# An attention-and-gate kernel: the fourth head pair's scores, maximum and exponentials moved ahead of batch 1's transposes in the opening list, and one copy of v rows moved from a DMA queue to GpSimd

## The chip, the core and the metric

The kernel runs on one core of a Trainium2 chip. The time is that of one execution on the device, in microseconds (us); a figure for a kernel is the median over its runs. The engines are named as in the profile: PE (TensorE matmul), PEld (TensorE weight load), DVE (VectorE), ACT (ScalarE), POOL (GpSimd), SP (SyncE, which here only issues DMAs).

## What is computed

The inputs are `q`, `k`, `v` of shape (8 batches, 8 heads, 576 positions, 64) and two weight matrices. Attention looks back over a window of 64 positions; its result, with the heads side by side, goes through two matrix products with a cosine gate between them.

```python
scores = q @ k.T / sqrt(64)                       # per batch and head
mask = (rel >= 0) & (rel < 64)                    # rel = row position - column position
scores = where(mask, scores, -1e9)
attn = exp(scores - max(scores)); attn = attn / (sum(attn) + 1e-9)
x = (attn @ v), heads side by side                # 4608 rows x 512
h = x @ w_in                                      # 512 -> 2048
out = (h * cos(h)) @ w_out                        # 2048 -> 512
```

## The kernel before

The 4608 rows are cut into nine macro-tiles of 512 rows (`MT`). For macro-tiles 1 to 8 a loop writes down the two big products (L458 for `x @ w_in`, L611 for the product with `w_out`), and a planner (`at`, `pump`) drops the attention steps of later tiles in between. Macro-tile 0 and the attention of batches 0 and 1 have no such cover yet. Their order is written out by hand in the string `FIRST`: a list of step names, emitted one after the other (L575). The list is the program order on each engine: every instruction that a step emits goes to the end of its engine's queue, and an engine takes its queue strictly in order, waiting on semaphores where data or buffers are not ready.

The names of the steps that matter here (`p` is a pair of heads, 0 to 3; `g` is 0 for the first four blocks of 64 positions of a pair, 1 for the next four):

| step | what it does | engine, line |
|---|---|---|
| `Lq1.x`, `Lk1.x`, `Lv0.x`, `Lwi.x` | loads of q and k of batch 1, of v of batch 0 (128 rows each), of a quarter of `w_in` | issued by POOL, L149, L172, L188 |
| `tq.p`, `tk.p` / `Tq.p`, `Tk.p` | 18 transposes of q or k of batch 0 / of batch 1 into PSUM | PE, L200 |
| `pq.p`, `pk.p` / `Pq.p`, `Pk.p` | copies of those transposes to SBUF, the last letter names the engine (`a` ACT, `d` DVE) | L121, L222, L224 |
| `s.p.g.bank` | scores of a group of four blocks: two matmuls that put the mask, then eight of q and k | PE, L304, L311 |
| `m.p.g` | row maximum of the group | DVE, L321 |
| `e.p.g` | four exponentials, each with its row sum | ACT, L338 |
| `i.p.g` | reciprocal of the row sums | DVE, L348 |
| `n.p.g.p` | exponentials times reciprocals, giving the weights `w` | POOL, L355 |
| `w.p.g`, `c.p.g` | four transposes of `w`, and their copy to SBUF | PE, L371; DVE or ACT, L121 |
| `zA`, `zB.0`, `zB.1`, `zC` | copies of half a v block into the odd slots of the v tile, 64 partitions each; `zB.0` and `zB.1` cover two slots (64x1024). The letter: `d` DVE, `s` a DMA from SP (L183), `p` POOL | |
| `v.a.g`, `x.a.g` | weights times v for two pairs (`a` is 0 or 1), and the copy into `xT` | PE, L408; L121 |
| `h.g.f.bank` | eight matmuls of `x @ w_in` | PE, L422 |
| `tb`, `S.g.f` | ACT's table load for the sine, and the sines | ACT, L453, L428 |
| `Gs.n`, `Gm.n` | scores and maximum of groups of batch 1 (numbers 9 to 12 here) | PE, L311; DVE, L326 |

`v.0.1` reads slots 3 and 5 of the v tile, whose lower halves `zB.0` fills and whose upper halves `zB.1` fills. `zB.0` needs the third and the fourth load of v (`Lv0.2`, `Lv0.3`), `zB.1` the second and the third. `zA` and `zC` fill slots 1 and 7. Waits between steps come from the data and from the buffers: the PSUM tiles with the tag `t` go round over three banks, and the scores, `h` and output tiles name their bank.

On PE the list runs, from the last transposes of batch 0 to the first `h`: `Tq.0 Tk.0 s.3.0 Tq.1 Tk.1 s.2.1 Gs.10 Gs.9 w.0.0 w.1.0 Gs.12 w.2.0 w.3.0 v.0.0 s.3.1 v.1.0 Gs.11 w.0.1 w.1.1 h.0.0 h.0.1 w.2.1 h.0.2 v.0.1 w.3.1 h.0.3`. On POOL, after the loads: `n.1.0 n.0.0 n.2.0 n.3.0 n.0.1 n.1.1 n.2.1 Lwi.3 n.3.1`.

Of the kernel before, what the change touches and what calls it, by code (L numbers as in the profile page):

```python
# [10 lines left out]
def _safe_warn(msg, *a, **kw):  # L11
# [30 lines left out]


FIRST = (
# [18 lines left out]
)  # L63


# [585 lines left out]
```

## Time and profile before

| | |
|---|---|
| median of 3 runs | 306.01 us (305.65 to 306.83) |
| the profiled execution | 306.57 us, of which the span from the first to the last instruction is 304.8 us |
| PE busy | 293.2 us, 96% of the span |
| ACT, DVE, POOL busy | 233.7, 217.4, 195.8 us |
| DMA moved | 41.44 MB, 136 GB/s in the mean |

Times in the views are microseconds from the start of the span. A row of the timeline gives the start, the time that its instructions took together, engine, line, operation, `out<-in`, shape and count; in brackets stands the idle time of the engine just before it and what ended it. Rows of equal operations that follow each other are merged. Matmuls are pipelined, so that the starts, not the durations, tell how fast PE goes. A wait for several semaphores is put down to the one that the profile saw last.

### The profile page before, as it was taken

What the parts mean: (1) busy time and instruction counts of PE and PEld (TensorE: products, weight loads), DVE (VectorE), ACT (ScalarE), POOL (GpSimd) and SP (SyncE); (2) the same over time, 40 slices, a digit from 0 to 9 for tenths busy, and PEclk for the clock granted to TensorE, in tenths of its full rate; (3) what the DMA queues carried; (4) which work ended last, traced back from release to release, by engine and by line L of the source; (5) the groups of instructions that cost most, each with busy time, mean ns of one, the idle gap of its engine ahead of it and who ended that gap; (6) DMA issues with size and microseconds to landing.
All of it is one profiled execution on the core that took longest, in us unless ns stands there. A gap on an engine that the chain in (4) does not pass through costs nothing.

```text
span 304.8 us, 8261 instructions
## 1 busy us (share of the span) xinstructions
PE 293.2 (96%) x2840; PEld 154.4 (51%) x2840; DVE 217.4 (71%) x868; ACT 233.7 (77%) x783; POOL 195.8 (64%) x226
## 2 busy tenths in 40 slices
PE   3789999999999999999999999999999999999995
PEld 3667854644455445444544444444544454454443
DVE  3797888898888877787678867886778677236701
ACT  5998699878986799779976998699869986116500
POOL 8899568986999579985998599769804930000000
PEclk9999999999999999999999999999999999999999
DMA  7999999999979995999999999999996852011011
GB/s 144 175 203 184 196 189 142 103 132 169 232 115 115 228 147 80 106 153 233 133 116 150 223 138 109 128 235 148 107 123 147 139 120 98 0 71 69 3 69 69
DMA packets 158186, 41.44 MB, mean 136 GB/s; under 512 B 146944, under 2 KB 153408, under 8 KB 158144
## 3 DMA queue, kind: packets, MB, share of 16 engines
q0 software_dynamic: 100192, 18.06, 80.8%
q1 hardware_dynamic: 57808, 22.66, 40.7%
q8 instruction: 22, 0.36, 0.5%
q14 instruction: 20, 0.16, 0.2%
q10 hardware_dynamic: 144, 0.20, 0.2%
HBM read 36.70 MB, written 9.44 MB: 151 GB/s over the span
## 4 chain that ended last, share of the span: by engine, by line
PE 90%; DVE 3%; DMA 2%; POOL 2%; ACT 1%; issue 1%; POOLq 0%
PE h_ps L458 37%; PE out_ps L611 36%; PE out_ps L441 5%; PE h_ps L422 4%; PE s_ps L289 3%; PE o_ps L390 3%; DMA k<-in_k_dram 2%; PE tq_ps L203 1%; PE out_ps L470 1%; DVE negm L321 1%; POOL q L149 1%; PE s_ps L311 1%; POOL k L149 1%; ACT e L338 0%; DVE wT L121 0%
## 5 line engine op out<-in xcount | busy, mean ns | idle before, releaser
L458 PE MATMUL h_ps<-xT,w_in 128*128 128x512 bf16 x512 | 115.1, 379 | 0.2
L611 PE MATMUL out_ps<-w_out,gT 128*128 128x512 bf16 x496 | 110.0, 379 | 0.0
L600 DVE TENSOR_TENSOR gT<-h_ps,sin 128x512 bf16<-128x512 f32 x128 | 85.1, 688 | 29.3 <-ACT sin L597 28.7
L338 ACT ACTIVATE e<-s,negm 128x128 f32<-128x128 f32 (+1 forms) x256 | 97.2, 382 | 1.7 <-POOL v L121 1.0
L597 ACT ACTIVATE sin<-h_ps 128x512 f32<-128x512 f32 x128 | 73.8, 598 | 31.4 <-PE h_ps L458 30.8
L355 POOL TENSOR_TENSOR w<-e,rden 128x512 bf16<-128x512 f32 (+1 forms) x68 | 69.3, 1033 | 30.8 <-DVE rden L348 25.0
L458 PEld LDWEIGHTS <-w_in 128*128 128x128 bf16 x512 | 48.9, 98 | 54.7
L611 PEld LDWEIGHTS <-gT 128*128 128x128 bf16 x496 | 47.4, 98 | 56.1
L326 DVE CUSTOM_DVE_ANT_0 s<-s_ps,mask 128x128 f32<-128x128 f32 (+1 forms) x256 | 56.1, 277 | 1.7 <-PE s_ps L311 1.4
L338 ACT ACTIVATION_READ_ACCUMULATOR e<-s,negm 128x1 f32 x256 | 48.3, 189 | 0.0
L172 POOL DMA_DIRECT2D v<-in_v_dram x40 | 34.1, 870 | 1.0 <-DMA q<-in_q_dram 1.0
L166 POOL DMA_DIRECT2D q<-in_q_dram x36 | 28.7, 797 | 7.6 <-DMA v<-in_v_dram 2.5
L166 POOL DMA_DIRECT2D k<-in_k_dram x36 | 28.5, 792 | 6.4 <-DMA k<-in_k_dram 4.5
L121 ACT COPY out_sb<-out_ps 128x512 f32<-128x512 f32 (+1 forms) x16 | 9.0, 563 | 23.9 <-PE out_ps L611 18.4
L348 DVE RECIPROCAL rden<-den 128x4 f32<-128x4 f32 (+1 forms) x73 | 12.2, 167 | 19.4 <-ACT e L338 19.0
L121 POOL COPY v<-v 64x1536 bf16<-64x1536 bf16 (+3 forms) x16 | 22.9, 1433 | 0.4
L121 DVE COPY out_sb<-out_ps 128x512 f32<-128x512 f32 x20 | 13.7, 687 | 12.1 <-PE out_ps L611 12.0
L121 DVE CAST xT<-o_ps 128x512 bf16<-128x512 f32 x24 | 15.6, 679 | 8.6 <-PE o_ps L390 8.4
L326 DVE DVE_READ_ACCUMULATOR2_ANT negm<- 128x1 f32 x256 | 21.3, 83 | 0.1
L441 PE MATMUL out_ps<-w_out,gT 128*128 128x512 bf16 x64 | 14.8, 380 | 0.0
L422 PE MATMUL h_ps<-xT,w_in 128*128 128x256 bf16 x128 | 14.6, 273 | 0.0
L422 PEld LDWEIGHTS <-w_in 128*128 128x128 bf16 x128 | 12.3, 98 | 1.4
(67 smaller groups left out, 230.9 us busy)
## 6 DMA issues: line engine op xcount, KB each, us to landing
out_dram<-out_sb SPq DMA_DIRECT2D x16, 512.0 KB, 7.3
v<-in_v_dram POOLq DMA_DIRECT2D x32, 128.0 KB, 6.0
q<-in_q_dram POOLq DMA_DIRECT2D x36, 96.0 KB, 8.7
k<-in_k_dram POOLq DMA_DIRECT2D x36, 96.0 KB, 8.6
w_in<-in_moe_w_in_dram POOLq DMA_DIRECT2D x4, 512.0 KB, 9.2
w_out<-in_moe_w_out_dram POOLq DMA_DIRECT2D x4, 512.0 KB, 11.0
q<-in_q_dram POOLq DMA_DIRECT2D x7, 144.0 KB, 6.5
k<-in_k_dram POOLq DMA_DIRECT2D x7, 144.0 KB, 6.7
```

Source lines behind the costliest of these rows:

```text
L121: {"a": nc.scalar.copy, "p": nc.gpsimd.tensor_copy}.get(engine, nc.vector.tensor_copy)(out, in_)
L166: nc.gpsimd.dma_start(out=st[name, b][:, c].rearrange("p (h d) -> p h d", h=H), in_=src.rearrange("h p d -> p h d"))
L172: nc.gpsimd.dma_start(out=vt.rearrange("p (h d) -> p h d", h=H), in_=v[b, :, c * 128:c * 128 + n, :].rearrange("h p d -> p h d"))
L326: nc.vector.tensor_tensor_reduce(out=s[:, u, c], in0=s_ps[:, u, c], in1=mask[:, 2 - j % 2 if j else 0, c], scale=-scale if b else -1.0, sc ...
L338: nc.scalar.activation(e[:, u, c], s[:, u, c], AF.Exp, bias=negm[:, u:u + 1], scale=1.0 if n < n_first else -1.0, accum_out=den[:, u:u + 1])
L355: (nc.gpsimd if engine == "p" else nc.vector).tensor_tensor(out=w[:, 0:u], in0=e[:, 0:u], op=ALU.mult, in1=rden[:, 0:u].unsqueeze(2).to_br ...
L422: nc.tensor.matmul(out=h_ps[:, half * e:half * e + half], lhsT=w_in_sb[:, ks, ff * 128:ff * 128 + 128], rhs=st["xT", 0][:, ks, half * g:ha ...
L441: nc.tensor.matmul(out=st["out", m], lhsT=st["g", ff // 2][:, ff % 2, m * 128:m * 128 + 128], rhs=w_out_sb[:, ff], start=ff == 0, stop=ff ...
L458: nc.tensor.matmul(out=st["h", ff], lhsT=w_in_sb[:, ks, ff * 128:ff * 128 + 128], rhs=st["xT", mt][:, ks], start=start, stop=stop)
L597: nc.scalar.activation(sin, h_ps, AF.Sin, bias=math.pi / 2.0)
L600: nc.vector.tensor_tensor(out=gt[:, e], in0=h_ps, in1=sin, op=ALU.mult)
L611: nc.tensor.matmul(out=o_ps[e], lhsT=gT[ff // 2][:, ff % 2, ms * 128:ms * 128 + 128], rhs=w_out_sb[:, ff], start=ff == 0, stop=ff == n_ff - 1)
```

## The change

Four steps of the list move ahead of neighbours, and one letter changes.

- `i.0.0` goes ahead of `pk.3.d` and `m.2.0` (DVE).
- `s.3.0.0` goes ahead of `Tk.0` (PE).
- `m.3.0` goes ahead of `Pq.0.d` and `i.1.0` (DVE).
- `e.3.0` goes ahead of `Pk.0.a` (ACT).
- `zB.0.s` becomes `zB.0.p`: the copy of v rows of slots 3 and 5, lower halves, is one POOL copy of 64x1024 instead of a DMA from SP. In POOL's queue it stands between `n.3.0` and `n.0.1`; in SP's queue `zB.1` is now the first of these copies.

The instructions are otherwise the same, in number too: PE keeps its 5682, and the list is written on one line less, so that later lines of the changed kernel have numbers lower by one.

```diff
 FIRST = (
...
-    "... Tq.0 Lv0.2 pk.3.d m.2.0 e.0.1 pq.3.a i.0.0 e.1.0 Tk.0 s.3.0.0 Tq.1 e.2.0 Lv0.3 Lwi.0 "
-    "Pq.0.d i.1.0 Lwi.1 m.3.0 m.1.1 i.2.0 Pk.0.a e.3.0 Lwi.2 Tk.1 n.1.0.p s.2.1.1 Pq.1.d ..."
+    "... Tq.0 Lv0.2 i.0.0 pk.3.d m.2.0 e.0.1 pq.3.a e.1.0 s.3.0.0 Tk.0 Tq.1 e.2.0 Lv0.3 Lwi.0 m.3.0 "
+    "Pq.0.d i.1.0 Lwi.1 m.1.1 i.2.0 e.3.0 Pk.0.a Lwi.2 Tk.1 n.1.0.p s.2.1.1 Pq.1.d ..."
...
-    "... n.3.0.p i.0.1 c.1.0.d zA.1.d c.2.0.d e.2.1 zB.0.s zB.1.s n.0.1.p i.1.1 w.3.0 v.0.0 ..."
+    "... n.3.0.p i.0.1 c.1.0.d zA.1.d c.2.0.d e.2.1 zB.0.p zB.1.s n.0.1.p i.1.1 w.3.0 v.0.0 ..."
...
 )
```

35 rows, old and new, of the table FIRST are left out of this document.

## The prediction

> **What bounds the kernel now.** I read the busy times first, then everything that PE waits for in the whole span (total, times, longest).
>
> ```profile
> PE 293.2 (96%) x2840; PEld 154.4 (51%) x2840; DVE 217.4 (71%) x868; ACT 233.7 (77%) x783; POOL 195.8 (64%) x226
> ...
> PE tq_ps L200 <- DVE q L121: 4.2, 1, 4.2
> PE tk_ps L200 <- issue: 1.4, 1, 1.4
> PE tw_ps L371 <- POOL w L355: 1.1, 2, 0.9
> PE o_ps L408 <- ACT small L453: 0.6, 1, 0.6
> ```
>
> PE is the bound, and after its start its listed waits are few and all in the opening. The end therefore moves by as much as PE's last wait of the opening moves. PE's timeline shows where that is:
>
> ```profile
> 12.62 0.37 PE L200 MATMUL tk_ps<-ident,k 64*64 64x64 bf16 x11 [0.26 <-DMA k<-in_k_dram]
> 14.45 0.28 PE L200 MATMUL tk_ps<-ident,k 64*64 64x64 bf16 x7 [1.45 <-issue]
> 14.78 0.36 PE L311 MATMUL s_ps<-kT,qT 64*64 64x64 bf16 x8
> 15.77 0.75 PE L311 MATMUL s_ps<-kT,qT 64*64 64x128 bf16 x22
> 17.46 0.62 PE L371 MATMUL tw_ps<-ident,w 128*128 128x128 bf16 x8 [0.94 <-POOL w L355]
> ...
> 19.50 0.40 PE L371 MATMUL tw_ps<-ident,w 128*128 128x128 bf16 x4 [0.19 <-POOL w L355]
> ...
> 21.57 0.62 PE L371 MATMUL tw_ps<-ident,w 128*128 128x128 bf16 x8
> 22.03 1.91 PE L422 MATMUL h_ps<-xT,w_in 128*128 128x256 bf16 x16
> 23.78 0.39 PE L371 MATMUL tw_ps<-ident,w 128*128 128x128 bf16 x4
> 24.00 1.04 PE L422 MATMUL h_ps<-xT,w_in 128*128 128x256 bf16 x8
> 25.63 0.44 PE L408 MATMUL o_ps<-wT,v 128*64 128x64 bf16 x16 [0.59 <-ACT small L453]
> ```
>
> The last wait is that of `v.0.1` at 25.63. From start to start eight `h` matmuls take (23.78 - 22.03)/2 = 0.875, so PE could have begun `v.0.1` at 24.00 + 0.875 = 24.875: the wait costs 0.755, more than the 0.59 in the bracket, which counts from a pipelined end. The bracket names ACT's table load, of which `v.0.1` reads nothing. It reads v slots that SP's transfers fill; their issue, and the time to landing of the first and of the second:
>
> ```profile
> 18.17 2.18 SPq L183 DMA_DIRECT2D v<-v  x3
> v<-v SPq DMA_DIRECT2D x1, 128.0 KB, 5.7
> v<-v SPq DMA_DIRECT2D x1, 128.0 KB, 6.6
> ```
>
> `zB.0` lands at 18.17 + 5.7 = 23.9; `zB.1`, issued a third of 2.18 later, at 18.9 + 6.6 = 25.5. That is the release of 25.63.
>
> The other runner is POOL, which feeds the transposes of `w`:
>
> ```profile
> 8.98 3.53 POOL L172 DMA_DIRECT2D v<-in_v_dram  x4 [0.74 <-DMA q<-in_q_dram]
> 14.55 0.74 POOL L188 DMA_DIRECT2D w_in<-in_moe_w_in_dram  x1 [0.55 <-DMA q<-in_q_dram]
> 15.37 6.13 POOL L355 TENSOR_TENSOR w<-e,rden 128x512 bf16<-128x512 f32 x6
> 21.97 1.04 POOL L355 TENSOR_TENSOR w<-e,rden 128x512 bf16<-128x512 f32 x1 [0.47 <-DVE rden L348]
> ```
>
> Six multiplies run without a gap from 15.37 to 21.50, 1.022 each. They start when `Lwi.2` is issued, and that waits for an earlier load's landing: nothing that the change touches.
>
> **Part 1: scores, maximum and exponentials of pair 3 earlier.** The same instructions move past one another, so only the order counts. The rows of DVE and ACT there:
>
> ```profile
> 12.64 0.68 DVE L321 TENSOR_REDUCE negm<-s_ps 128x4 f32<-128x512 f32 x1
> 13.32 0.73 DVE L121 COPY qT<-tq_ps 128x576 bf16<-128x576 bf16 x1
> 13.96 0.17 DVE L348 RECIPROCAL rden<-den 128x4 f32<-128x4 f32 x1
> 15.19 1.29 DVE L321 TENSOR_REDUCE negm<-s_ps 128x4 f32<-128x512 f32 x2 [1.06 <-PE s_ps L311]
> 17.72 0.17 DVE L348 RECIPROCAL rden<-den 128x4 f32<-128x4 f32 x1
> 14.85 0.68 ACT L121 COPY kT<-tk_ps 128x576 bf16<-128x576 bf16 x1
> 15.92 0.37 ACT L338 ACTIVATE e<-s_ps,negm 128x128 f32<-128x128 f32 x1 [0.39 <-DVE negm L321]
> 17.30 0.65 ACT L121 COPY kT<-tk_ps 128x576 bf16<-128x576 bf16 x1
> ```
>
> Before, `s.3.0` stood behind the 1.45 us gap inside `Tk.0` and ran at 14.78. Now it stands in front of `Tk.0`. The gap waits for no semaphore of the program; whether it belongs to a place in PE's instruction stream, to a time near 13.0 or to `Tk.0` itself, the ten matmuls of `s.3.0` come before it (by place, with only two instructions to spare: they and one transposition with its weights fill the stretch that eleven transpositions filled). The last copy of k that they need ends as `m.2.0` begins, near 12.7, so the scores are done near 13.0.
>
> DVE: `m.2.0` ends at about 13.32, shifted to 13.4 by `i.0.0`; `m.3.0` then takes 0.59 (half of the two at 15.19, start to start 0.6) to 14.0, `Pq.0` 0.64 to 14.65, `i.1.0` follows at 14.65 instead of 13.96. `n.1.0` needs it at 15.37: 0.6 of cover, cost nothing. `i.3.0` waits for `e.3.0` and comes near 16.8 instead of 17.72.
>
> ACT: `e.3.0` runs at 14.85 in `Pk.0`'s place, (17.30 - 15.92) = 1.38 long, to 16.23; `Pk.0` and `Pk.1`, at most 0.65 each, to 16.85 and 17.4. ACT loses its 0.39 wait, but `Pk.0` is 1.4 later, and queued behind it on PE stand the scores of group 10 (from about 16.0 to 16.9) and group 9. The 14 matmuls of both are part of the 22 at 15.77 and take about 0.4, to 17.3. PE waits for POOL until 17.46 anyway: the cover is 0.15 thick. If it is gone, each further tenth shows at 17.46, but the 0.19 of idle before 19.50, where POOL is again last, takes that up.
>
> So part 1 removes PE's wait for nobody: at 17.46 and 19.50 the multiplies on POOL end last, before and after. Worth 0.0; bounds -0.05 and +0.1.
>
> **Part 2: `zB.0` on POOL.** Adds one copy to POOL's chain, before `n.0.1`. POOL's copies of v elsewhere in the kernel:
>
> ```profile
> L121 POOL COPY v<-v 64x2048 bf16<-64x2048 bf16 x5 | 9.5, 1894 | 0.3
> L121 POOL COPY v<-v 64x1024 bf16<-64x1024 bf16 x4 | 4.1, 1036 | 0.1
> L121 POOL COPY v<-v 64x512 bf16<-64x512 bf16 x2 | 2.0, 1012 | 0.1
> ```
>
> The same shape is there: 1.036. Its data (`Lv0.3`, issued last of four from 8.98, landing at 18.1 since SP's issue at 18.17 waited for it) are in place before its turn at 15.37 + 4 x 1.022 = 19.46. `n.1.1` then ends at 21.50 + 1.03 = 22.53. Queued behind: `n.2.1` ends near 23.6 instead of 23.0 (its wait of 0.47 for DVE absorbs half), PE needs it only at 24.55; `n.3.1`, after the issue of `Lwi.3` (0.8, as at 14.55), ends near 25.4 and is needed behind `v.0.1`, at 26.0. `w.0.1` has its `n.0.1` at 21.51, just in time. PE needs `n.1.1` for `w.1.1`, in the middle of the eight transposes at 21.57, that is at 21.80. With the 0.04 that lay between the end of `n.3.0` and PE's start at 19.50, `w.1.1` starts at 22.57 and `h.0.0` at 22.57 + (22.03 - 21.57)/2 = 22.80: 0.77 later than before.
>
> On SP, `zB.1` is now first and needs only the second and third v load. A load takes this long:
>
> ```profile
> v<-in_v_dram POOLq DMA_DIRECT2D x2, 128.0 KB, 6.5
> w_in<-in_moe_w_in_dram POOLq DMA_DIRECT2D x1, 512.0 KB, 12.4
> ```
>
> The third is issued at 8.98 + 2 x 0.88 = 10.74 and lands at 17.24. `zB.1` starts 1.65 earlier and lands at 17.24 + 5.7 to 6.6 = 22.9 to 23.8. PE comes to `v.0.1` at 22.80 + (24.00 - 22.03) + 0.875 = 25.65. The copy is there, the wait of 0.755 is gone, and `v.0.1` starts at 25.65 instead of 25.63.
>
> **Sum.** +0.77 (waiting for POOL) - 0.755 (no wait for SP's transfer) + 0.0 = +0.02. Behind 25.65 PE's order is the same and it has no listed wait. Against the profiled execution (306.57, span 304.8 and 1.77 around it): 306.6. The median of the runs is 0.56 lower; on that scale 306.0.
>
> **Rules weighed.** Of DVE's two equal copies of v rows, `zA`, one took 0.74, the other 0.29:
>
> ```profile
> 17.80 0.74 DVE L121 COPY v<-v 64x512 bf16<-64x512 bf16 x1
> 19.30 0.29 DVE L121 COPY v<-v 64x512 bf16<-64x512 bf16 x1
> ```
>
> The first started in the middle of POOL's third multiply and ended 0.1 after it (15.37 + 3 x 1.022 = 18.44); so the two engines can hold each other up. [...] In my sum both `zA` are done before 19.46, since DVE runs nearly 0.9 earlier from `i.3.0` on. What it would cost otherwise is the first rival.
>
> **Rivals.** *The copy on POOL is longer (0.15).* For: 64x512 took 1.012 where half the step from 1024 to 2048 leaves 1.036 - 0.43 = 0.61, so those two were held up by 0.4; against: the four of 64x1024 were not. Price 0.3 to 0.86 (as long as 2048 takes), all on PE's path at `w.1.1`: 306.3 to 306.9.
>
> *The gap catches the scores (0.05).* If the gap falls ahead of `s.3.0`'s last matmul, they end at 14.5, `m.3.0` at 15.1, and `Pq.0` and `i.1.0`, now behind `m.3.0`, at 15.9: `n.1.0` starts 0.6 late and the whole chain of POOL with it: 306.6. It decides from two instructions on.
>
> *`zB.1` lands late (0.05), the slower side.* It starts in the stage in which `w_in` loads are queued, and one of those took 12.4. From 25.65 - 17.24 = 8.4 to landing PE waits again at `v.0.1`; at 9.9 it costs 1.5, at 12.4 it costs 4.0: 307.5 to 310. Against: 5.7 and 6.6 of its own kind.
>
> *PE slows down after idling (0.03).* The same two mask matmuls took 0.62 at the start of the kernel and 0.38 soon after:
>
> ```profile
> 9.31 0.62 PE L304 MATMUL s_ps<-mask,ident 64*64 64x512 bf16 x2
> 10.49 0.38 PE L304 MATMUL s_ps<-mask,ident 64*64 64x512 bf16 x2
> ```
>
> So PE begins slower. A second slow stretch as long as the one from PE's start at 4.2 to 9.31 would cost (1 - 0.38/0.62) of 5.1 = 2.0: 308.0. Against: after the gap of 1.45 the transposes came at full pace, and the new wait at 21.80 is 0.77. [...]
>
> *A gain (0.08).* By the slope alone the copy costs 0.86, giving 305.8; if it were wholly hidden, PE would reach `v.0.1` at 24.88, giving 305.3. No row shows POOL idle there.
>
> **The numbers.** The forecast of no change has 0.64. A measurement can tell about 0.5% here, 1.53 us. Slower by more than that takes the late landing or the slow clock, 0.05 + 0.03; faster would need nearly all of PE's waits from 17.46 on (0.94 + 0.19 + 0.755), for which I leave 0.03, of the gain's 0.08; the rest, 0.89, lies within. The range goes from the gain (305.6 in its middle) less the 0.36 by which the lowest run undercut the median, to the dear copy (306.9) plus 0.3: 305.2 to 307.2.
>
> **What would show it.** Right: `s.3.0` before the gap; POOL's copy at 19.46 with about 1.03; a PE wait for POOL `w` of 0.7 before the transposes at 22.6; no wait at `v.0.1`, near 25.65; the block of 96 `h` matmuls at 27.6. Wrong: a wait left at `v.0.1`, a copy over 1.3, multiplies that start after 15.4 without a late load, or new waits after 28.

## The result, and the profile after

| | before | after |
|---|---|---|
| median of 22 runs each, side by side | 306.19 us (305.59 to 307.54) | 307.41 us (306.51 to 312.22) |
| ratio | | 1.0037 (95%: 1.0023 to 1.0052) |
| the profiled execution, and its span | 306.57 us, 304.8 us | 306.51 us, 304.7 us |
| start of the block of 96 `h` matmuls | 27.58 us | 27.67 us |

The change makes the kernel a little slower: 0.2 to 0.5%, above the 307.2 at which the forecast's range ended. The profiled execution of after is the fastest of its 22 runs, so its trace shows what the change does to the order, but not the loss. Of the 22 runs of after the one of 312.22 counts as slow (more than 1.5% above the fastest), and such runs are left out of the ratios and means here, but not out of the medians and the counts.

The busy times on the page of after:

```profile
PE 290.6 (95%) x2807; PEld 154.8 (51%) x2840; DVE 217.9 (72%) x868; ACT 233.4 (77%) x783; POOL 196.4 (64%) x227
```

What its PE waits for (total, times, longest):

```profile
PE tq_ps L199 <- DVE q L120: 4.2, 1, 4.2
PE s_ps L310 <- ACT kT L120: 1.8, 2, 1.5
PE out_ps L610 <- issue: 1.7, 11, 0.2
PE tk_ps L199 <- issue: 0.7, 1, 0.7
PE o_ps L407 <- DVE v L120: 0.5, 1, 0.5
```

POOL has one instruction more (227), the copy. The waits for POOL's `w` and at `v.0.1` (0.6 for ACT in the view of before) have left the list; a wait of 1.5 for ACT's copy of k and one of 0.5 for DVE's copy of v are new. (The 11 short "issue" gaps stand where matmul records are missing: 2807 of 2840.) PE's timeline of after, in the opening:

```profile
13.04 0.39 PE L310 MATMUL s_ps<-kT,qT 64*64 64x64 bf16 x8
...
14.17 0.44 PE L199 MATMUL tk_ps<-ident,k 64*64 64x64 bf16 x17 [0.74 <-issue]
...
17.37 0.55 PE L310 MATMUL s_ps<-kT,qT 64*64 64x128 bf16 x14 [1.46 <-ACT kT L120]
17.85 0.62 PE L370 MATMUL tw_ps<-ident,w 128*128 128x128 bf16 x8
...
20.41 0.38 PE L407 MATMUL o_ps<-wT,v 128*64 128x64 bf16 x12 [0.47 <-DVE v L120]
...
22.79 1.91 PE L421 MATMUL h_ps<-xT,w_in 128*128 128x256 bf16 x16
...
25.72 0.44 PE L407 MATMUL o_ps<-wT,v 128*64 128x64 bf16 x16
...
27.67 10.65 PE L421 MATMUL h_ps<-xT,w_in 128*128 128x256 bf16 x96
```

`s.3.0` runs at 13.04, ahead of the gap in `Tk.0`, as forecast. `w.0.0` starts at 17.85, but now PE comes to it late: until 17.37 it has waited for ACT's copy of k. `h.0.0` starts at 22.79 (forecast 22.80) and `v.0.1` at 25.72 without a wait (forecast 25.65; from the start of eight `h` matmuls to `v.0.1` it is 0.97 here, where the forecast took 0.875). Beside it POOL's and DVE's timelines of after:

```profile
15.09 4.08 POOL L354 TENSOR_TENSOR w<-e,rden 128x512 bf16<-128x512 f32 x4
19.11 1.03 POOL L120 COPY v<-v 64x1024 bf16<-64x1024 bf16 x1
20.11 2.13 POOL L354 TENSOR_TENSOR w<-e,rden 128x512 bf16<-128x512 f32 x2
...
16.91 0.35 DVE L120 COPY v<-v 64x512 bf16<-64x512 bf16 x1
19.14 1.21 DVE L120 COPY v<-v 64x512 bf16<-64x512 bf16 x1
```

The copy took the 1.03 that was forecast. DVE's second `zA`, 0.29 before, begins 0.03 after it and ends 0.2 after it: 1.21. PE's 0.47 at 20.41 is the wait for that.

### The profile page after: what moved, and what is told of

The parts are those of the page before. It is cut to its first block, busy times and chain, and to the rows that moved or that the text cites. A ratio compares the mean times of both kernels' runs of the same rounds, so it can differ in the third digit from the quotient of the medians.

```text
span 304.7 us, 8228 instructions
## 1 busy us (share of the span) xinstructions
PE 290.6 (95%) x2807; PEld 154.8 (51%) x2840; DVE 217.9 (72%) x868; ACT 233.4 (77%) x783; POOL 196.4 (64%) x227
## 4 chain that ended last, share of the span: by engine, by line
PE 92%; DVE 2%; ACT 2%; issue 2%; DMA 1%; SPq 0%
PE h_ps L457 36%; PE out_ps L610 35%; PE h_ps L421 5%; PE out_ps L440 4%; PE s_ps L288 3%; PE o_ps L389 3%; ACT e L337 1%; PE s_ps L310 1%; PE tq_ps L202 1%; PE out_ps L469 1%; DMA rows<-in_k_dram 1%; PE tk_ps L199 1%; PE tw_ps L370 1%; PE tq_ps L199 1%; DVE s L325 1%
## 5 line engine op out<-in xcount | busy, mean ns | idle before, releaser
L610 PE MATMUL out_ps<-w_out,gT 128*128 128x512 bf16 x482 | 107.3, 379 | 1.9 <-issue 1.7
L354 POOL TENSOR_TENSOR w<-e,rden 128x512 bf16<-128x512 f32 (+1 forms) x68 | 69.3, 1032 | 27.9 <-DVE rden L347 22.8
L120 POOL COPY v<-v 64x1024 bf16<-64x1024 bf16 (+3 forms) x17 | 23.9, 1408 | 0.4
L440 PE MATMUL out_ps<-w_out,gT 128*128 128x512 bf16 x60 | 14.3, 380 | 0.3 <-issue 0.2
```

Source lines behind the costliest of these rows:

```text
L120: {"a": nc.scalar.copy, "p": nc.gpsimd.tensor_copy}.get(engine, nc.vector.tensor_copy)(out, in_)
L354: (nc.gpsimd if engine == "p" else nc.vector).tensor_tensor(out=w[:, 0:u], in0=e[:, 0:u], op=ALU.mult, in1=rden[:, 0:u].unsqueeze(2).to_br ...
L440: nc.tensor.matmul(out=st["out", m], lhsT=st["g", ff // 2][:, ff % 2, m * 128:m * 128 + 128], rhs=w_out_sb[:, ff], start=ff == 0, stop=ff ...
L610: nc.tensor.matmul(out=o_ps[e], lhsT=gT[ff // 2][:, ff % 2, ms * 128:ms * 128 + 128], rhs=w_out_sb[:, ff], start=ff == 0, stop=ff == n_ff - 1)
```

## The experiments

The theories. **A**, clock and ACT: with `e.3.0` ahead of `Pk.0` PE idles for ACT, and its clock then falls in part of the runs. **B**, the copy: POOL's chain is on the path and the credit at `v.0.1` is not regular. **C**, the hold-up: POOL's copy holds up `zA.1`, and that is the loss. **D**: nothing but the spread between runs. Below, "low clock" counts runs whose granted clock, in the mean over the span, was at most 0.996.

| kernel | what it has of the change | ratio to before (95%) | low clock |
|---|---|---|---|
| after again / b / c | all | 1.0012 (0.999 to 1.0034) / 1.0013 (0.9994 to 1.0033) / 1.0013 (0.9992 to 1.0034) | 4, 6, 3 of 12 |
| before again | nothing | 0.9996 (0.9966 to 1.0027) | 1 of 12 |
| order only | the order | 1.0009 (0.9977 to 1.004) | 6 of 12 |
| copy only | the copy | 1.0009 (0.9985 to 1.0034) | 2 of 12 |
| pk first | all but `e.3.0` ahead of `Pk.0` | 1.0022 (0.9997 to 1.0047) | 0 of 12 |
| swap only | only `e.3.0` ahead of `Pk.0` | 1.0025 (1.0003 to 1.0047) | 5 of 12 |
| filled / b / c | all, and PE kept busy | 1.0001 (0.9985 to 1.0017) / 0.9999 (0.998 to 1.0018) / 1.001 (0.9989 to 1.0031) | 0, 0, 0 of 12 |
| zA early | all, `zA.1` ahead of the copy | 1.001 (0.9984 to 1.0036) | 5 of 12 |
| order, filled | the order, and PE kept busy | 1.0025 (1.0005 to 1.0046) | 1 of 12 |
| zB swap | none; `zB.1` ahead of `zB.0` on SP | 1.001 (0.999 to 1.003) | 0 of 12 |
| copy doubled | `zB.0` and `zB.1` on POOL | 1.0095 (1.0062 to 1.0128) | 5 of 9 |
| scores only | `i.0.0`, `s.3.0`, `m.3.0` early | 1.0017 (0.9991 to 1.0043) | 0 of 12 |

Single ratios of 0.1% are below what these runs tell apart; the traces and the counts carry more.

**Both kernels again, and each half alone.** The first is the changed kernel, the last the kernel before, each unedited; the two in the middle take one half of the change:

```diff
 # order only
-    "... e.2.1 zB.0.p zB.1.s n.0.1.p ..."
+    "... e.2.1 zB.0.s zB.1.s n.0.1.p ..."
 # copy only: the order of before, and in it
-    "... e.2.1 zB.0.s zB.1.s n.0.1.p ..."
+    "... e.2.1 zB.0.p zB.1.s n.0.1.p ..."
```

> The changed kernel once more, beside the others. Known so far: its median is 0.37% (1.1 us) over the kernel before, while its profiled execution, at 306.51 the lowest of its 22 runs, reaches the block of 96 h matmuls at 27.67, only 0.09 later than before. Theory O (the order on ACT and PE): with k's copies behind e.3.0, PE stands still for 1.46 in front of groups 10 and 9, and in part of the runs PE then goes slower for a stretch; theory P (the copy on POOL): DVE's second copy of v rows waits for POOL's copy, how long depends on who comes first, and in part of the runs v.0.0 is late by more than the 0.47 of the profiled one. Both expect 307.0 to 307.8 here and a spread of over 1.5; a typical execution should show the lost time, for O as matmuls at half pace, for P as a PE wait for DVE of 1 us or more near 20.

> Only the order is changed (i.0.0, s.3.0, m.3.0 and e.3.0 earlier); zB.0 stays a transfer of SP. Theory O: the loss is here, ratio 1.003 to 1.006, some granted clocks below 1. Theory P: no loss, 0.998 to 1.001, since POOL's chain is as before; by the terms of the prediction for this part 0.0 us.

> Only zB.0 goes to POOL; the order is as before. Theory P: the loss is here, ratio 1.002 to 1.006. Theory O: 0.999 to 1.001, as by the prediction's terms for this part (+0.77 of waiting for POOL, -0.755 of waiting for SP's transfer). With DVE later than in the changed kernel, its second copy of v rows may meet POOL's copy or not; the start of v.0.0 and of v.0.1 tells.

> The kernel before as a control: ratio 1.000 within 0.1%, spread below 1 us in most runs. Theory O expects granted clocks of nearly 1 in all its runs, theory P makes no difference between the clocks of the two kernels.

Neither half carries the loss alone (both 1.0009), and the repeat of after lost less than the first measurement. The traces say more. In the timeline of PE in copy only, `w.1.1` waits for POOL as forecast, and `v.0.1` waits for nothing:

```profile
22.17 0.40 PE L366 MATMUL tw_ps<-ident,w 128*128 128x128 bf16 x4 [0.57 <-POOL w L350]
22.41 1.91 PE L417 MATMUL h_ps<-xT,w_in 128*128 128x256 bf16 x16
...
25.34 0.44 PE L403 MATMUL o_ps<-wT,v 128*64 128x64 bf16 x16
```

But in the second profile of the kernel before, `v.0.1` doesn't wait either; here are PE's rows, and SP's issue:

```profile
21.42 1.91 PE L422 MATMUL h_ps<-xT,w_in 128*128 128x256 bf16 x16
...
24.18 1.05 PE L422 MATMUL h_ps<-xT,w_in 128*128 128x256 bf16 x8 [0.63 <-DVE negm L326]
25.16 0.44 PE L408 MATMUL o_ps<-wT,v 128*64 128x64 bf16 x16
...
17.42 2.43 SPq L183 DMA_DIRECT2D v<-v  x3
```

SP's transfers began at 17.42, against 18.17 in the profile on which the prediction rests, and `v.0.1` had no wait for them. The wait that this execution has instead, 0.63 for DVE's maximum, is another one.

**The swap of `e.3.0` and `Pk.0`, and PE kept busy.** For the changed kernel with the swap undone, the kernel before with the swap alone, the changed kernel with six extra mask matmuls on PE ahead of group 10's scores (they write a bank that is written again right after; nothing is left out), and the changed kernel with `zA.1` earlier:

```diff
 # pk first: of the changed kernel
-    "... i.2.0 e.3.0 Pk.0.a Lwi.2 ..."
+    "... i.2.0 Pk.0.a e.3.0 Lwi.2 ..."
 # swap only: of the kernel before
-    "... i.2.0 Pk.0.a e.3.0 Lwi.2 ..."
+    "... i.2.0 e.3.0 Pk.0.a Lwi.2 ..."
 # filled: of the changed kernel, in g_scores
-        if n == FILL[1]:
+        for _ in range(6 if n == 10 else n == FILL[1]):
 # zA early: of the changed kernel
-    "... w.1.0 c.0.0.d ... c.1.0.d zA.1.d c.2.0.d ..."
+    "... w.1.0 zA.1.d c.0.0.d ... c.1.0.d c.2.0.d ..."
```

> The changed kernel with one move undone: ACT copies k of batch 1 (Pk.0) ahead of e.3.0 again; scores and maximum of pair 3 stay early, zB.0 stays on POOL. In the three profiles with the moved order PE stood 1.3 to 1.5 us for that copy ahead of groups 10 and 9, and the granted clock was at or below 0.995 in 20 of 46 runs with that order against 7 of 59 without it. Theory O (PE's longer idle time, late start and slow stretch come from this move): PE's wait for ACT's copy of k falls below 0.6, at most 3 of 12 runs at such a clock, median 0.4 to 1 us below the changed kernel, ratio 0.998 to 1.002. Theory P (the copy on POOL is the loss): the wait goes too, but the ratio stays at 1.002 to 1.005.

> The kernel before with only e.3.0 put ahead of Pk.0 on ACT. Theory O: 4 or more of 12 runs at a clock of 0.995 or less, PE waits over 1 us for the copy of k, ratio 1.001 to 1.005. Theory P, or a theory that the early scores on PE matter: 0 to 2 such runs, ratio 0.999 to 1.001.

> The changed kernel with six more matmuls of the mask on PE (512 columns each, some 1.3 us together) ahead of group 10's scores, written where the scores overwrite them: PE is busy in the time in which it waited for the copy of k, and nothing else is added. Theory O in the form that the idle time lowers the clock: at most 2 of 12 runs at 0.995 or less, median 0.2 to 0.6 us below the changed kernel. If the slow clock had another cause, 4 or more such runs and the median of the changed kernel, 307.4, or above.

> The changed kernel with DVE's second copy of v rows (zA.1) put ahead of c.0.0, into the 0.7 to 1.0 us in which DVE waits for PE's transposes of w. In the changed kernel's profile that copy took 1.21 instead of 0.29, beside POOL's copy of v rows, and v.0.0 then waited 0.47. Theory P (the two copies hold each other up): it takes 0.3 to 0.5 here, no PE wait at v.0.0, median 0.3 to 0.6 us below the changed kernel. Theory O alone: the row gets short as well, but the runs stay as they are, 4 or more of 12 at a clock of 0.995 or less and a ratio of 1.001 to 1.004.

PE's timeline of swap only:

```profile
17.36 0.55 PE L306 MATMUL s_ps<-kT,qT 64*64 64x128 bf16 x14 [2.02 <-ACT kT L116]
17.85 0.86 PE L366 MATMUL tw_ps<-ident,w 128*128 128x128 bf16 x8
...
19.53 0.61 PE L366 MATMUL tw_ps<-ident,w 128*128 128x128 bf16 x4
19.93 0.63 PE L364 MATMUL tw_ps<-ident 128*128 128x128 bf16 x4
...
20.92 0.64 PE L403 MATMUL o_ps<-wT,v 128*64 128x64 bf16 x16
```

PE waits 2.02 for ACT's copy, and after that its rows come slower up to 21.5: four transposes 0.61 where they take 0.40, sixteen matmuls of v 0.64 instead of 0.44. With the swap undone (pk first) PE's timeline at this place is like that of before again, with the wait back at POOL:

```profile
15.25 0.83 PE L306 MATMUL s_ps<-kT,qT 64*64 64x128 bf16 x22
16.93 0.62 PE L366 MATMUL tw_ps<-ident,w 128*128 128x128 bf16 x8 [0.85 <-POOL w L350]
```

No run of pk first had the low clock; its 1.0022 is nevertheless what theory B expected, though its interval also holds no loss at all.

The view by stretches sets the granted clock beside PE's busy time: length, busy time of PE, PEld, DVE, ACT, POOL, then the granted clock, DMA share, GB/s. Swap only:

```profile
14.67:18.08 3.41, 1.39 (x43) 1.08 (x37) 2.69 (x7) 3.41 (x18) 3.35 (x4) 1.00 1.72 192
18.08:21.50 3.42, 3.06 (x43) 2.47 (x41) 2.22 (x8) 2.57 (x16) 2.92 (x4) 0.50 1.23 204
```

Filled, where the extra matmuls lie in the gap:

```profile
12.99:16.41 3.42, 2.53 (x72) 1.77 (x68) 3.42 (x9) 3.30 (x19) 3.35 (x5) 1.00 2.25 164
16.41:19.82 3.41, 3.41 (x62) 2.25 (x60) 2.52 (x10) 3.41 (x19) 3.41 (x4) 1.00 1.28 206
```

And after, the profile of the result:

```profile
14.85:18.27 3.42, 1.86 (x54) 1.54 (x51) 2.42 (x7) 3.42 (x18) 3.31 (x5) 1.00 1.72 187
18.27:21.68 3.41, 2.78 (x60) 1.98 (x60) 3.30 (x12) 2.98 (x15) 3.41 (x4) 1.00 1.22 215
```

These stretches are cut in steps of 3.413 us from the moment at which a trace's record of the clock begins. In the opening PE is slow up to a moment (11.26 in swap only, 11.44 in after; between 8.8 and 13.1 in all) at which its rows become fast and the record of the clock begins (in after b at 11.03: eighteen transposes take 0.74 at 9.83 and 0.47 at 11.11). Every later change in the records lies a whole number of stretches of 3.413 us behind that moment: in swap only 6.82 and 10.24 behind 11.26, at 18.08 and 21.50; in the first profile of before the record stands at 1.00 from 10.36 for 293.546, which is 86 stretches. In the four traces with a low clock the clock stays full for two stretches and is then 0.50 for exactly one. In the stretch just before it PE was busy 1.39 (swap only), 1.59 (order only), 1.64 (zA early) and 1.73 (after b) of 3.41; in the fifteen other traces that have the record no stretch of the opening has less than the 1.86 of after. So in these traces the drop went with how the stretches happened to fall on PE's wait. If a stretch of 3.41 is slid through a profile, the share of the positions in which it would hold less than 1.8 is an estimate of how often the clock falls; beside it stands the count of runs with the low clock:

| kernels | estimate | counted |
|---|---|---|
| `e.3.0` ahead of `Pk.0`, PE not filled (after and its repeats, order only, swap only, zA early) | 0.40, mean of seven profiles | 39 of 94 |
| before (its runs beside the experiments) | 0.11, mean of four profiles | 13 of 137 |
| copy doubled, below | 0.47, one profile | 5 of 9 |
| filled three times; order, filled | 0 | 1 of 48 |
| copy only, pk first, zB swap, scores only | 0 | 2 of 48 |

With the bound at 1.74 or 1.86, the two ends that the traces leave open, the 0.40 is 0.35 or 0.51. Theory A holds as to the clock, with the swap as the main cause and PE's idle time as the way (the low clock in 39 of 94 runs unfilled, in 1 of 48 filled). It needs no ACT: in copy doubled PE waits for POOL (1.12 and 0.60), and before has the gap inside `Tk.0`, with which its first profile comes down to 1.70 in some positions.

Theory C falls in part. In zA early both `zA` are done before POOL's copy begins (1.49 for the two, beside its multiplies), and PE's wait at `v.0.0` is gone; yet 1.001 can't be told from after's 1.0012 to 1.0013.

**The order filled, the credit, POOL's chain, the scores.**

```diff
 # order, filled: order only with the edit of "filled"
 # zB swap: of the kernel before
-    "... zB.0.s zB.1.s n.0.1.p ..."
+    "... zB.1.s zB.0.s n.0.1.p ..."
 # copy doubled: of the kernel before
-    "... zB.0.s zB.1.s n.0.1.p ..."
+    "... zB.0.p zB.1.p n.0.1.p ..."
 # scores only: the changed kernel with zB.0.s, and
-    "... i.2.0 e.3.0 Pk.0.a Lwi.2 ..."
+    "... i.2.0 Pk.0.a e.3.0 Lwi.2 ..."
```

> The moved order with zB.0 left to SP, and the six extra mask matmuls on PE ahead of group 10's scores. With the copy on POOL the same filling gave 306.89 and no run at a low clock. Theory O: again 0 to 2 of 12 at 0.995 or less. If the copy on POOL costs about 0.4 besides (runs at full clock: mean 307.19 with it over 61 runs, 306.77 without it over 85), the median is 306.3 to 306.7 here, ratio 0.998 to 1.000; if it costs nothing, 306.9 as with it.

> The kernel before with SP's two transfers exchanged: zB.1 first, which waits for earlier loads, then zB.0. Both still go through SP. If v.0.1's wait for the later transfer (0.755 in the profile of before) is a cost in most runs, this brings zB.1's landing ahead by about 1.6 and leaves zB.0's 0.7 later, ratio 0.998 to 0.999; if that wait is only what PE is early by in some runs, 0.9995 to 1.001. It also bounds what the change could have gained at v.0.1 at all.

> The order of before, and both zB.0 and zB.1 as copies of POOL, one after the other ahead of n.0.1: the suspected cost doubled. Theory P: with v.0.1's wait already gone, the second copy's 1.03 lies whole on PE's path through n.1.1 and w.1.1, so that the wait for POOL ahead of w.1.1 grows from 0.57 to about 1.6, median 307.6 to 308.2, ratio 1.003 to 1.006. If POOL's chain is not what PE waits for in most runs: below 1.002.

> Only i.0.0, s.3.0 and m.3.0 earlier; ACT's order (k's copy ahead of e.3.0) and the transfer on SP as before. With the copy on POOL this was 307.11, ratio 1.0022, without any run at a low clock. If the copy on POOL is what remains there: 0.999 to 1.001 here. If the early scores cost by themselves (Tq.1 and Tk.1 come later on PE, which now waits 0.4 for DVE ahead of Tk.1): 1.001 to 1.003. Low clocks: 0 to 2 of 12 in both cases.

zB swap starts the transfer that ended last first. `v.0.1` has no wait in its profile and nothing is gained (1.001): putting that transfer first does not bring the 0.755. Copy doubled shows that POOL's chain to `w.1.1` is on the path, in PE's timeline:

```profile
21.94 0.40 PE L366 MATMUL tw_ps<-ident,w 128*128 128x128 bf16 x4 [1.12 <-POOL w L350]
22.94 0.40 PE L366 MATMUL tw_ps<-ident,w 128*128 128x128 bf16 x4 [0.60 <-POOL w L350]
23.18 1.91 PE L417 MATMUL h_ps<-xT,w_in 128*128 128x256 bf16 x16
```

Two copies cost PE 1.72 there where one cost 0.57. The kernel's 0.95%, above the 0.3 to 0.6% that were expected, is in part the clock: its four runs at full clock have a mean of 307.97 against 306.49 of before (0.5%), its five others 310.40. The two other kernels say that the order without the swap (1.0017), or with PE filled (1.0025), is no gain either. Order, filled speaks against theory B: its median of 306.93 is the one that was expected if the copy on POOL costs nothing, beside the 306.89 of filled, which has the copy.

**After and filled once more, in turn.** Still open was whether filling gives the whole loss back; both went again, twice each, and then the kernel before twice for its profile.

> The changed kernel, beside its filled version on the same chip (each twice, to be pooled). Theory O alone (the slow stretch of the clock is the whole loss): about 40% of the runs at 0.995 or less, ratio 1.002 to 1.004, and the runs at full clock are at the level of the kernel before, within 0.1%. Theory O with a rest: the runs at full clock are 0.3 to 0.6 us above the kernel before as well.

> The changed kernel with six extra mask matmuls on PE ahead of group 10's scores. Theory O alone: at most 2 of 12 runs at a low clock, ratio 0.999 to 1.001. Theory O with a rest (POOL's copy in the chain to w.1.1, no wait at v.0.1 to set against it): ratio 1.001 to 1.002, with a PE wait for POOL of about 0.6 ahead of w.1.1 in the profile.

> As the other run of the changed kernel in this group: to be pooled with it.

> As the other run of the filled kernel in this group: to be pooled with it.

Taken together, 24 runs of after against 35 of before give 1.0018 (1.0009 to 1.0028), 24 of filled 1.0006 (0.9995 to 1.0017). Of the 24 of after, nine had the low clock, with a mean of 307.17; the fifteen others still have 306.92 against the 306.42 of before at full clock. So the clock is not all of it; nor is it the spread alone (theory D), since the interval of after and that of the first measurement leave out 1. The fence shows POOL's timeline in the third repeat of after:

```profile
15.97 4.08 POOL L354 TENSOR_TENSOR w<-e,rden 128x512 bf16<-128x512 f32 x4 [1.27 <-DVE rden L347]
```

Here `n.1.0` had to wait 1.27 for `i.1.0`, which the change put behind `m.3.0`. The second repeat had DVE's `zA.1` against POOL's copy again:

```profile
18.81 1.24 DVE L120 COPY v<-v 64x512 bf16<-64x512 bf16 x1
```

> One more profile of the kernel before. If the wait at v.0.1 is regular: PE idle 0.4 or more there, v.0.1 near 25.6. If it was an accident of the first profile: none, v.0.1 between 24.6 and 25.3, as in the second profile of this kernel (25.16).

> A further profile of the kernel before, for the same question: a wait of 0.4 or more at v.0.1 if it is regular, none if it was an accident of the first profile.

One run each, 305.65 and 307.14 us. From the first, PE's, POOL's and SP's timelines:

```profile
21.15 1.91 PE L422 MATMUL h_ps<-xT,w_in 128*128 128x256 bf16 x16
...
24.09 0.44 PE L408 MATMUL o_ps<-wT,v 128*64 128x64 bf16 x16
...
26.20 10.65 PE L422 MATMUL h_ps<-xT,w_in 128*128 128x256 bf16 x96
...
14.47 6.12 POOL L355 TENSOR_TENSOR w<-e,rden 128x512 bf16<-128x512 f32 x6
...
16.97 2.55 SPq L183 DMA_DIRECT2D v<-v  x3
```

And from the second:

```profile
24.67 0.44 PE L408 MATMUL o_ps<-wT,v 128*64 128x64 bf16 x16
...
17.77 2.27 SPq L183 DMA_DIRECT2D v<-v  x3
```

Neither waits at `v.0.1`. With this the account can be made in two stretches that leave out how early an execution's loads landed, but also what delays POOL's first multiply: I, from that multiply to `h.0.0`; II, from `h.0.0` to the block of 96.

| profiles | I | II |
|---|---|---|
| before, four executions | 6.66, 6.96, 6.68, 6.77 | 5.55, 5.76, 5.05, 5.05 |
| one copy on POOL, full clock (after, its first and third repeat; copy only, pk first, filled three times) | 7.70, 7.44, 7.41; 7.42, 7.41, 7.41, 7.45, 7.48 | 4.88 to 4.89 |
| early scores without the copy, full clock (scores only; order, filled) | 7.11; 7.24 | 4.88; 4.89 |
| zB swap | 6.86 | 5.36 |
| low clock (order only, swap only, zA early, after b) | 7.97, 8.01, 7.90, 8.07 | 4.88 to 4.89 |
| copy doubled | 8.66 | 4.88 |

Stretch I is 0.71 longer with the copy, in profile after profile (the median of the eight is 7.43, that of the four 6.72). Not all of that is the copy where the order is moved too: without it I is 7.11 and 7.24 there, with a stop of PE of 0.38 and 0.52 in `s.3.1` that the last section shows. The copy alone is copy only's 7.42. Stretch II is shorter by 0.67 only in the execution that the prediction was made from, by 0.88 in another, which had the wait for DVE, and by 0.17 in the two others: 0.47 in the mean. In scores only and order, filled it is as short without the copy. I and II together are 11.73 to 12.72 in before, 12.29 to 12.58 with one copy at full clock, and 11.99 and 12.13 in those two. At the low clock stretch I is 7.99 in the mean, 0.56 over the 7.43, and the same with the copy or without: there PE itself ends last.

## Why the prediction was wrong

It said 306.0 with nothing won or lost. Three steps failed.

**The credit, "-0.755 (no wait for SP's transfer)".** The debit beside it, +0.77, was nearly right: 0.71 in stretch I, and so were its parts (copy 1.03 as forecast; `w.1.1` waits 0.57 in copy only and the third repeat). The credit was read from one execution in which SP began at 18.17. In three others it began at 16.97 to 17.77 and `v.0.1` didn't wait. A wait that comes in one execution of four had been set against a cost that comes in all; and even there it was 0.67 in stretch II and not 0.755, since from the start of eight `h` matmuls to `v.0.1` it takes 0.97 where nothing waits. In the mean of the four profiles 0.71 - 0.47 = 0.24 is left as a loss. The debit and the missing wait are shown in the traces; the mean of 0.47 rests on four profiles alone, and one of these four is longer over both stretches than any with one copy at full clock.

**The cover on PE, "0.15 thick", and the rival "PE slows down after idling", 0.03.** The 0.15 was counted from POOL's end at 17.46. In every profile with the swap and without the filling PE stands 1.26 to 2.02 for ACT's copy, where the kernels without it wait for ACT 0.7 at most at a time: the path to `w.0.0` went from POOL to ACT, and `w.0.0` came late. That alone would be little, as the prediction said. But with the longer idle stretch the clock fell in 4 runs of 10 (39 of 94), and that rival had been put aside for a wrong reason: "after the gap of 1.45 the transposes came at full pace" is one execution, in which that gap fell on two stretches of the clock and left PE busy 2.38 and 2.08 of 3.41 in them. With the swap it was 1.39 to 1.73 in the profiles that lost the clock. The longest wait before a drop was 2.02 (swap only), and the granted clock was 0.50 over the next 3.41. The changes lie on a grid of 3.413 us that begins at another moment in each execution (10.36 in the first profile of before, 11.44 in after), so that the same wait falls on it in different ways. Price: 0.56 in stretch I; among the runs with the swap, 307.60 in the mean at the low clock against 307.09, 0.5 (0.17 to 1.53 within the single launches). The forecast's 2.0 was too dear: the slow stretch lasts 3.41 and not 5.1, and POOL's waits take up a part.

**The cover on DVE, "0.6 of cover, cost nothing".** `i.1.0` stands behind `m.3.0` now, and `n.1.0`, POOL's first multiply, starts some 0.33 after it where it waits for it. In six of the twelve profiles with this order POOL waits there: 0.17 and 1.27 in two repeats of after, 0.83 in order only, 0.46 in zA early, 0.35 in pk first, 0.82 in the second of filled. In the profile of after the cover was used up too (`i.1.0` at 14.76, `n.1.0` at 15.09). The mean is 0.33 over the twelve, against 0.09 over the eight with DVE's order of before (none in its four profiles, 0.29 in zB swap, 0.39 in copy doubled). The two stretches leave this out; how much of the 0.24 between them reaches the end is not shown.

Together: 0.24 + 0.4 x 0.56 = 0.46 us, and at most 0.24 more from DVE, against 0.56 measured with the last repeats (1.0018) and 1.1 in the first measurement (1.0037). The sum fits the repeats, but their times don't show the parts one by one. Filled, which has the copy and DVE's order, loses 0.19; the runs of after at full clock lose 0.50; and scores only and order, filled lose 0.17 and 0.25% without the copy. That each half alone costs its share is likewise no more than consistent with the runs: 1.0009 with an interval that holds 0.28 us as well as nothing. Most of the loss in the first measurement isn't the clock either: the twelve of its runs at full clock have a mean of 307.37, 0.96 above the 306.41 of before. What that was stays open. The spread behind the block of 96 is large enough to hide such amounts: the rest of the span, with the same instructions, takes 277.2 to 278.7 in the four executions of before and 277.0 to 279.2 in all, and PE's waits for transfers of `w` are up to 1.0 of it (zB swap).

Smaller points. *"Both `zA` are done before 19.46"* was wrong: the second met POOL's copy and took 1.21 and 1.24. Beside POOL's multiplies a `zA` took between 0.27 (copy only) and 1.14 (scores only). The hold-up shows in after's stretch I, 7.70 against the median of 7.43. Removing it (zA early) did not show in the time. *Right*: `s.3.0` ahead of the gap, no wait at `v.0.1`, `zB.1` never late, no new waits behind 28. *What would make it wrong* had named late multiplies, which came in the third repeat (15.97), but neither the credit nor the clock: in the profile of after every date from 22.8 on came out as forecast, and the forecast of the time was wrong all the same, since the date it was compared with, 25.63, was a late one.

## What to carry to other kernels

A credit and a debit that cancel need a second profile of the kernel before: ask of each whether it comes in every execution; a cover of a tenth read from one trace is no cover. Measure such stretches from an event inside, not from the span's start, since the loads' landing moves everything (SP's transfers, which wait for it, began at 16.97 to 18.17 in the four profiles of before); and choose one that the change itself doesn't move, which POOL's first multiply here was not. Where PE is already half idle, don't lengthen its waits, even off the path, without filling them: here the clock fell after stretches of 3.41 us in which PE was busy 1.39 to 1.73 and not after 1.86 and more, while the longest single wait did not decide it (the clock fell with waits of 1.26 and 1.29 and stayed full with one of 1.46). Six spare matmuls kept it in 47 of 48 runs, though here no version beat the kernel before.

## What the runs showed of the hardware

- The granted clock changed on a grid of 3.413 us that began at another moment in each execution (8.8 to 13.1). In the opening it fell to 0.50 for one such stretch after one in which PE was busy 1.39 to 1.73 us (four profiles), and stayed full after 1.86 and more (fifteen). With waits of 1.26 to 2.02 in the opening that came to 39 of 94 runs; filled (2.3 and more), to 1 of 48. One lost stretch, half of 3.413 in 305, is 0.0056 of the mean clock of a run: most low runs show 0.993 or 0.994, a few 0.989, as two would give.
- In several kernels PE stops for nothing that the profile names, in the scores matmuls `s.3.1`. PE's timeline in the first repeat of after, and then in order, filled:

```profile
19.55 0.33 PE L310 MATMUL s_ps<-kT,qT 64*64 64x128 bf16 x6
20.59 0.24 PE L310 MATMUL s_ps<-kT,qT 64*64 64x128 bf16 x2 [0.71 <-issue]
```

```profile
20.82 0.41 PE L306 MATMUL s_ps<-kT,qT 64*64 64x128 bf16 x8 [0.52 <-issue]
```

In the first it stands behind the sixth of eight matmuls, as in pk first (0.54) and scores only (0.38); in the second, which has six more matmuls ahead, six matmuls earlier. So it belongs to a place in PE's stream and not to a time or a step, though some executions, the profile of before among them, don't show it. The gap in `Tk.0`, whose nature the prediction had left open, is of the same kind: before and after the change it comes behind the same number of PE's matmuls (11 of `Tk.0`, or ten of `s.3.0` and one of `Tk.0`). From it to the stop in `s.3.1` the timelines count 128 matmuls, each with one load of weights, in either order and with the filling. What stops PE there, no run shows.
